# x and v of step 1 loaded three units ahead, sums written over v, small filter tables placed behind E

## The chip, the cores and the metric

The kernel runs on one core of a Trainium2 chip. The metric is device time in microseconds (us); the median of three runs of the kernel before is 1146.1 us (1141.72 to 1146.43). Engines are named as in the profile: PE (TensorE matmul), PEld (its weight loads), DVE (VectorE), ACT (ScalarE), POOL (GpSimd), SP (SyncE, which issues nearly all DMAs of this kernel; SPq is its queue).

## The reference

Two parts, the second fed by the first. All in float32.

```python
# x, v: (4, 11456, 128); pos_emb: (11456, 64); w1: (64, 64); w2: (64, 128)
h = (np.maximum(pos_emb @ w1, 0) @ w2) * np.exp(-0.01 * pos)[:, None]   # a filter
y = irfft(rfft(x * v, 2S, axis=1) * rfft(h, 2S, axis=0))[:, :S]         # long convolution
a = (x * y).reshape(B * S, D)                                           # 45824 tokens
logits = a @ phi                                                        # 32 slots, 8 experts
slot_in = softmax(logits, axis=0).T @ a
slot_out = per expert: relu(slot_in @ w1[e]) @ w2[e]
return softmax(logits, axis=1) @ slot_out
```

## The kernel before

The convolution is a transform of length 111 x 197, done as matrix products in float32. The 128 channels are worked in 8 groups of 16; with 4 batches a group has 64 columns, handled as 16 *units* of 4 columns.

- **Opening** (group-free): 14 loads `pos` feed `hid_step` (the small network of the filter), then `first` with the table `tab1h`, then `filter_second`. The small tables `tab1h`, `w1s`, `w2s`, `wins` are used only up to `filter_last` in group 0.
- **Step 1**, per unit u of group g: `p1_load` loads x and v (224 KB each), multiplies them (POOL, in group 0 every third on DVE), and makes the sum and the difference of the two halves on DVE (`sd`, two instructions, L203). `p1` multiplies sd by `tab1x` on PE (L126, 8 PE instructions a unit) and the result is brought to T, mainly by ACT (L130, L131, L135).
- **Step 2** (`p2`, per 4 frequencies k): a product with W (L218), two multiplications with the filter on DVE (L223), two combinations on POOL (L229, L230) back into T.
- **Step 3** (`p3`, two calls a unit, 16 PE instructions a unit, L236): a product from T, one copy `ec` by ACT (L240) and two DVE instructions into E (L242) a call.
- **Step 4** (`p4`, 7 row blocks, each in two halves): a product of E (L266), multiplied by the gate's x (`xi`, loaded by L254) on DVE (L272) into `xo`, stored to DRAM by `p4_out` (L286, L290, L298).
- After the eight groups the expert part (`Moe`, `_moe`) reads the stored tokens back; the change does not touch its text.

The main loop (L304) runs *passes* g = 0 to 8. A pass has two halves. In the first half step 1 of group g runs unit by unit beside step 3 of group g-1; p1 of a unit writes the places of T that p3 of the same unit reads. In the second half step 4 of group g-1 runs beside step 2 of group g. Pass 0 has no steps 3 and 4, pass 8 no steps 1 and 2.

What sets the order: each engine executes its instructions in the order of its own queue. A scheduler fills the queues when the kernel is built: among the instructions whose inputs and buffers it reckons to be free it takes the one that stands earliest in the text. `inorder` (`tc.keep_in_program_order`) pins an instruction behind the one written before it on the same engine. SP's queue waits at its head: a DMA whose buffer is not free holds back every DMA behind it.

Buffers that matter: pool `ld` has 5 buffers of 2 KB a partition and serves `pos`, x, v (from group 1 on) and `xi`; pool `st` has 3, for `hb` in the opening, sd and `xo`. In group 0 v lies in Hs, a region that the filter values of the later groups use (`hs`, loaded for group g in units 4 to 12 of pass g). E is a region of 15910 floats a partition, of which the steps use 14336 and the opening (hid, F and a ring) 15085. Step 1 is started two units ahead: `p1_load(g, u + 2)` stands before p3 and p1 of unit u.

Of the kernel before, what the change touches and what calls it, by code (L numbers as in the profile page):

```python
# [11 lines left out]
F32 = mybir.dt.float32  # L12
# [5 lines left out]
B, S, D = 4, 11456, 128  # L18

N1, N2 = 111, 197  # L20
L = N1 * N2
J = 99
JT = 105
JP = 112
R = 56
RP = 64
FO = 64
# [32 lines left out]
def conv_part(ctx, tc, cp, moe, xf, vf, xi, pos, w1, w2, win, t1x, t1h, wt, t3, t4, hs, scr):  # L60
    nc = tc.nc
    ld = ctx.enter_context(tc.tile_pool(name="ld", bufs=5))
    st = ctx.enter_context(tc.tile_pool(name="st", bufs=3))
    sm = ctx.enter_context(tc.tile_pool(name="sm", bufs=2))
    psa = ctx.enter_context(tc.tile_pool(name="psa", bufs=4, space=bass.MemoryType.PSUM))
    psb = ctx.enter_context(tc.tile_pool(name="psb", bufs=4, space=bass.MemoryType.PSUM))

    tab1x = cp.tile([JT, 2 * J], F32, tag="tab1x", name="tab1x")
    tab1h = cp.tile([J, 2 * J], F32, tag="tab1h", name="tab1h")
    tab3 = cp.tile([N1, 4 * R], F32, tag="tab3", name="tab3")  # L70
    tab4 = cp.tile([J, 2, N2 + JT], F32, tag="tab4", name="tab4")
    w1s = cp.tile([128, 2 * FO], F32, tag="w1s", name="w1s")
    w2s = cp.tile([128, D], F32, tag="w2s", name="w2s")
    wins = cp.tile([J, R, 2], F32, tag="wins", name="wins")
    W = cp.tile([128, J, N1], F32, tag="W", name="W")


# [3 lines left out]
    Hs = Tall[:, B * 2 * CG * J :].rearrange("p (k x) -> p k x", k=J)  # L81
    moe.E = cp.tile([128, QN * (NSLOT + 1) + 4096], F32, tag="E", name="E")
    E = moe.E[:, : 4 * C * R].rearrange("p (r q c) -> p r q c", q=4, c=C)
    inorder = tc.keep_in_program_order
    RB = 4
    KB = 4
# [98 lines left out]

    def p1_load(g, u):
        xt = ld.tile([JP, 4, 2 * RP], F32, tag="ld", name=f"x_{g}_{u}")
        dma = nc.sync.dma_start(out=xt, in_=xf[g, u])
        if g == 0:
            inorder(dma)  # L190
        if g == 0:

            k = 8 * RP * (u % 5)
            vt = Hs[:JP].rearrange("p k x -> p (k x)")[:, k : k + 8 * RP]
            vt = vt.rearrange("p (c r) -> p c r", c=4)
        else:
            vt = ld.tile([JP, 4, 2 * RP], F32, tag="ld", name=f"v_{g}_{u}")
        nc.sync.dma_start(out=vt, in_=vf[g, u])
        eng = nc.vector if g == 0 and u % 3 == 2 else nc.gpsimd
        inorder(eng.tensor_tensor(out=xt, in0=xt, in1=vt, op=ALU.mult))  # L200
        sd = st.tile([JP, 4, 2 * RP], F32, tag="st", name=f"sd_{g}_{u}")
        for h, op in ((0, ALU.add), (RP, ALU.subtract)):
            add = nc.vector.tensor_tensor(out=sd[:, :, h : h + RP], in0=xt[:, :, 0:RP], in1=xt[:, :, RP:],  # L203
                                          op=op)
            if g == 1:
                inorder(add)
        return sd

    def p1(g, u, sd):
        for h in range(0, 4, 2):  # L210
# [91 lines left out]
    NU = C // 4  # L302

    for g in range(G + 1):  # L304

        if g < G:
            sds = {u: p1_load(g, u) for u in range(2)}
            for u in range(NU):
                if g and 4 <= u < 13:
                    ks = slice(11 * (u - 4), 11 * (u - 3))  # L310
                    inorder(nc.sync.dma_start(out=Hs[:, ks], in_=hs[g, :, ks]))
                if u + 2 < NU:
                    sds[u + 2] = p1_load(g, u + 2)
                if g > 0:
                    p3(g - 1, 4 * u)
                    p3(g - 1, 4 * u + 2)
                p1(g, u, sds.pop(u))
        else:
            moe.weights()
            for u in range(NU):  # L320
                p3(g - 1, 4 * u)
                p3(g - 1, 4 * u + 2)
            moe.places()
# [520 lines left out]
```

## Time and profile before

| what | value |
|---|---|
| median of three runs | 1146.1 us |
| the profiled execution, its own time | 1144.67 us |
| its span (first to last instruction) | 1142.9 us |
| mean granted TensorE clock | 0.967 |
| opening and step 1 of group 0 | 0 to about 125 us |
| step 2 of group 0 | about 125 to 176 us |
| passes 1 to 7, first half / second half | about 52 us / 50 us each |
| pass 8 | about 883 to 937 us |
| expert part | about 937 us to the end |

A row of the timeline reads: start, duration, engine, line, operation, output<-inputs with partitions x elements, how many instructions were merged (x8), and in square brackets how long the engine had been idle and which instruction ended that. Consecutive instructions of a line are merged into one row if nothing of that engine came between. One float32 matmul of the text shows as two PE instructions. A row of the stages (windows) reads: stretch, its length, then busy time and number of instructions for PE, PEld, DVE, ACT and POOL, the granted clock, the busy share of the DMA engines, and GB/s. A row of the waits reads: engine, line, what it waited for: us in total, number of waits, the longest.

### The profile page before, as it was taken

Reading aid. Unit: us, or ns where it says so; the run is one execution under the profiler, and the core shown is the slowest. Engines: PE = TensorE matmul, PEld = TensorE weight load, DVE = VectorE, ACT = ScalarE, POOL = GpSimd, SP = SyncE. Lnnn points to the kernel's source line nnn. Section 1 sums busy time; section 2 is a strip of 40 time slices with the busy share of each in tenths; the row PEclk is TensorE's granted clock in tenths of the full one; section 3 lists DMA queues with packets and bytes.
Section 4 is the critical chain, followed back from the end, with each engine's and each line's share of the span. In section 5 each row is a group of like instructions: output and inputs, shape, how many; then the busy total and the mean of one; then the engine's idle time right before and its main releaser. Section 6 shows DMA issues by size and latency. Waiting matters only on the chain.

```text
span 1142.9 us, 25992 instructions
## 1 busy us (share of the span) xinstructions
PE 1065.8 (93%) x9232; PEld 990.3 (87%) x9232; DVE 878.7 (77%) x1806; ACT 594.7 (52%) x1473; POOL 589.6 (52%) x742
## 2 busy tenths in 40 slices
PE   6998998999999899999999999999999989987997
PEld 6787898999999899989989998998999986655775
DVE  5336667888779688877978787897888839997797
ACT  1978766901840590185049108604920318875697
POOL 6101465266447436743754574375456005776774
PEclk9779998999999999999999999999999989998999
DMA  8423577434824663483357247445824778774388
GB/s 281 132 81 89 183 263 222 146 107 136 237 90 125 184 190 94 141 215 109 117 173 219 76 131 214 127 125 162 231 80 150 234 232 264 228 209 123 137 346 342
DMA packets 129484, 198.44 MB, mean 174 GB/s; under 512 B 15927, under 2 KB 71538, under 8 KB 129357
## 3 DMA queue, kind: packets, MB, share of 16 engines
q1 hardware_dynamic: 129070, 196.61, 55.8%
q8 instruction: 75, 1.23, 0.5%
q14 instruction: 53, 0.43, 0.1%
q10 hardware_dynamic: 254, 0.11, 0.0%
q0 software_dynamic: 32, 0.07, 0.0%
HBM read 136.84 MB, written 59.90 MB: 172 GB/s over the span
## 4 chain that ended last, share of the span: by engine, by line
issue 32%; PE 22%; DVE 16%; DMA 6%; ACT 5%; POOL 3%; SPq 1%; POOLq 0%; DVEq 0%; ACTq 0%
PE p L126 7%; PE p L236 7%; DVE E L242 5%; DMA v<-in_vf_dram 5%; POOL x L200 2%; PE ct L702 2%; DVE xreg L413 2%; DVE sd L203 2%; PE p L266 1%; PE pt L472 1%; DVE xreg L718 1%; DVE ev L539 1%; DVE rd L492 1%; DVE c L679 1%; DVE rm L489 1%
## 5 line engine op out<-in xcount | busy, mean ns | idle before, releaser
L240 ACT ACTIVATE ec<-p 99x224 f32<-99x224 f32 x256 | 83.7, 356 | 396.6 <-issue 338.2
L242 DVE TENSOR_TENSOR E<-p,ec 99x224 f32<-99x224 f32 x512 | 222.3, 553 | 44.9 <-ACT ec L240 44.5
L229 POOL TENSOR_TENSOR T<-m,m 111x256 f32<-111x256 f32 (+1 forms) x200 | 145.2, 726 | 185.6 <-DVE m L223 184.1
L223 DVE TENSOR_TENSOR m<-p,T 111x512 f32<-111x512 f32 (+1 forms) x350 | 216.1, 679 | 23.4 <-issue 16.7
L236 PE MATMUL p<-tab,T 111*99 111x112 f32 x2048 | 222.2, 262 | 6.5 <-POOL T L229 3.0
L200 POOL TENSOR_TENSOR x<-x,v 112x512 f32<-112x512 f32 x112 | 145.0, 1296 | 158.3 <-DMA v<-in_vf_dram 145.4
L236 PEld LDWEIGHTS p<-tab,T 111*99 111x99 f32 x2048 | 215.4, 171 | 11.4 <-POOL T L229 3.2
L266 PE MATMUL p<-E,tab 99*105 99x128 f32 (+1 forms) x1792 | 212.6, 274 | 12.2 <-DVE E L242 12.2
L126 PE MATMUL p<-tab1x,sd 105*128 105x198 f32 x1024 | 201.3, 342 | 18.2 <-DVE sd L203 15.8
L266 PEld LDWEIGHTS p<-E,tab 99*105 99x105 f32 x1792 | 202.6, 172 | 14.4 <-DVE E L242 12.1
L218 PE MATMUL p<-T,W 128*111 128x128 f32 x1584 | 201.4, 279 | 1.1 <-DVE T L133 1.1
L126 PEld LDWEIGHTS p<-tab1x,sd 105*128 105x128 f32 x1024 | 172.1, 194 | 24.9 <-DVE sd L203 15.0
L218 PEld LDWEIGHTS p<-T,W 128*111 128x111 f32 x1584 | 189.8, 176 | 2.9 <-DVE T L133 1.3
L130 ACT ACTIVATE T<-p 64x396 f32<-64x396 f32 x288 | 163.8, 569 | 36.2 <-PE p L126 31.7
L203 DVE TENSOR_TENSOR sd<-x 112x256 f32<-112x256 f32 x256 | 116.2, 494 | 49.3 <-POOL x L200 39.9
L230 POOL TENSOR_TENSOR T<-m,m 111x256 f32<-111x256 f32 (+1 forms) x200 | 145.2, 726 | 0.0
L272 DVE TENSOR_TENSOR xo<-p,xi 105x256 f32<-105x256 f32 x224 | 84.1, 417 | 43.7 <-PE p L266 28.6
L131 ACT ACTIVATE T<-p 64x198 f32<-64x198 f32 x288 | 106.0, 368 | 3.5
L135 ACT ACTIVATE T<-p 64x198 f32<-64x198 f32 x224 | 74.3, 332 | 0.0
L133 DVE TENSOR_SCALAR T<-p 64x198 f32<-64x198 f32 x64 | 27.0, 431 | 45.4 <-ACT T L131 44.0
L520 POOL TENSOR_TENSOR E<-lt,mx 128x480 f32<-128x480 f32 (+1 forms) x24 | 24.6, 1024 | 70.0 <-ACT et L502 66.9
L706 ACT ACTIVATE cs<-ct 96x512 fp32r<-96x512 f32 x96 | 53.3, 567 | 10.2 <-PE ct L702 6.8
(94 smaller groups left out, 1128.3 us busy)
## 6 DMA issues: line engine op xcount, KB each, us to landing
x<-in_xf_dram SPq DMA_DIRECT2D x128, 224.0 KB
v<-in_vf_dram SPq DMA_DIRECT2D x112, 224.0 KB
xi<-in_xi_dram SPq DMA_DIRECT2D x112, 224.0 KB
out_dram<-xreg SPq DMA_DIRECT2D x22, 960.0 KB
xreg<-scr SPq DMA_DIRECT2D x21, 960.0 KB
scr<-xo SPq DMA_DIRECT2D x104, 192.0 KB
hs<-E SPq DMA_DIRECT2D x12, 1024.0 KB
T<-hs SPq DMA_DIRECT2D x63, 176.0 KB
```

The costliest lines, as they stand in the source:

```text
L126: nc.tensor.matmul(ps[:, i].rearrange("p s k -> p (s k)"), lhsT=src(i), rhs=tab, start=True, stop=True)
L130: nc.scalar.activation(to[0:RP], pq[0:RP], AF.Copy)
L131: nc.scalar.activation(to[RP:128, 0], pq[RP:128, 1], AF.Copy)
L200: inorder(eng.tensor_tensor(out=xt, in0=xt, in1=vt, op=ALU.mult))
L203: add = nc.vector.tensor_tensor(out=sd[:, :, h : h + RP], in0=xt[:, :, 0:RP], in1=xt[:, :, RP:], op=op)
L218: nc.tensor.matmul(ps[:, i].rearrange("p b c -> p (b c)"), lhsT=W[:, k0 + i, :], rhs=Tf[:, :, k0 + i, :], start=True, stop=True)
L223: nc.vector.tensor_mul(m[:, :n].rearrange("p k s c i -> p k (s c i)").rearrange("p k (b c) -> p k b c", c=CG), ps[:, :n], h[:, :, CG * s : ...
L229: nc.gpsimd.tensor_tensor(out=Ty[:, 0], in0=ms[0][:, :n, 0], in1=ms[1][:, :n, 1], op=ALU.subtract)
L230: nc.gpsimd.tensor_tensor(out=Ty[:, 1], in0=ms[1][:, :n, 0], in1=ms[0][:, :n, 1], op=ALU.add)
L236: nc.tensor.matmul(ps[:, i, 2 * s : 2 * s + 2, :].rearrange("p q r -> p (q r)"), lhsT=T[0:N1, s, c // CG, c % CG // 2, :, i], rhs=tab3[:, ...
L242: add = nc.vector.tensor_tensor(out=E[:J, :, 2 * s : 2 * s + 2, c : c + 2].rearrange("p r q c -> p c q r"), in0=ps[:, :, 0:2, :], in1=ec, ...
L266: nc.tensor.matmul(ps[:, i, :n], lhsT=tab4[:, s, o : o + JT], rhs=E[:J, r, s : s + 2 * n - 1 : 2, :], start=(s == 0), stop=(s == 1))
```

## The change

- `p1_load` is cut in two: `p1_load` issues the loads, `p1_fold` does the multiplication and the two sums. Loads stand three units ahead, the fold two units ahead as before. At the start of a pass the loads of units 0, 1 and 2 come first, then the folds of 0 and 1.
- Both loads are now pinned (`inorder`) in every group. Before, only x of group 0 was.
- From group 1 on, v is loaded into pool `st`; the sum and the difference are written over v, so that sd has no buffer of its own. In group 0 the same is done in Hs, with six places instead of five.
- Pool `st` has 5 buffers instead of 3.
- `tab1h`, `w1s`, `w2s`, `wins` are no longer tiles of their own; `spare` cuts them from the end of E, behind the ring.

```diff
-    st = ctx.enter_context(tc.tile_pool(name="st", bufs=3))
+    st = ctx.enter_context(tc.tile_pool(name="st", bufs=5))
...
-    tab1h = cp.tile([J, 2 * J], F32, tag="tab1h", name="tab1h")
-    w1s = cp.tile([128, 2 * FO], F32, tag="w1s", name="w1s")
-    w2s = cp.tile([128, D], F32, tag="w2s", name="w2s")
-    wins = cp.tile([J, R, 2], F32, tag="wins", name="wins")
...
+    at = count(J * N1 + 16 * 2 * D)
+
+    def spare(p, n):
+        a = next(at)
+        for _ in range(n - 1):
+            next(at)
+        return moe.E[:p, a : a + n]
+
+    tab1h = spare(J, 2 * J)
+    w1s = spare(128, 2 * FO)
+    w2s = spare(128, D)
+    wins = spare(J, 2 * R).rearrange("p (r h) -> p r h", h=2)
...
     def p1_load(g, u):
         xt = ld.tile([JP, 4, 2 * RP], F32, tag="ld", name=f"x_{g}_{u}")
-        dma = nc.sync.dma_start(out=xt, in_=xf[g, u])
-        if g == 0:
-            inorder(dma)
-        if g == 0:
-
-            k = 8 * RP * (u % 5)
+        inorder(nc.sync.dma_start(out=xt, in_=xf[g, u]))
+        if g == 0:
+
+            k = 8 * RP * (u % 6)
             vt = Hs[:JP].rearrange("p k x -> p (k x)")[:, k : k + 8 * RP]
             vt = vt.rearrange("p (c r) -> p c r", c=4)
         else:
-            vt = ld.tile([JP, 4, 2 * RP], F32, tag="ld", name=f"v_{g}_{u}")
-        nc.sync.dma_start(out=vt, in_=vf[g, u])
+            vt = st.tile([JP, 4, 2 * RP], F32, tag="st", name=f"v_{g}_{u}")
+        inorder(nc.sync.dma_start(out=vt, in_=vf[g, u]))
+        return xt, vt
+
+    def p1_fold(g, u, xt, vt):
+
         eng = nc.vector if g == 0 and u % 3 == 2 else nc.gpsimd
         inorder(eng.tensor_tensor(out=xt, in0=xt, in1=vt, op=ALU.mult))
-        sd = st.tile([JP, 4, 2 * RP], F32, tag="st", name=f"sd_{g}_{u}")
         for h, op in ((0, ALU.add), (RP, ALU.subtract)):
-            add = nc.vector.tensor_tensor(out=sd[:, :, h : h + RP], in0=xt[:, :, 0:RP], in1=xt[:, :, RP:],
+            add = nc.vector.tensor_tensor(out=vt[:, :, h : h + RP], in0=xt[:, :, 0:RP], in1=xt[:, :, RP:],
                                           op=op)
             if g == 1:
                 inorder(add)
-        return sd
+        return vt
...
-            sds = {u: p1_load(g, u) for u in range(2)}
+            xvs = {u: p1_load(g, u) for u in range(3)}
+            sds = {u: p1_fold(g, u, *xvs.pop(u)) for u in range(2)}
             for u in range(NU):
                 if g and 4 <= u < 13:
                     ks = slice(11 * (u - 4), 11 * (u - 3))
                     inorder(nc.sync.dma_start(out=Hs[:, ks], in_=hs[g, :, ks]))
+                if u + 3 < NU:
+                    xvs[u + 3] = p1_load(g, u + 3)
                 if u + 2 < NU:
-                    sds[u + 2] = p1_load(g, u + 2)
+                    sds[u + 2] = p1_fold(g, u + 2, *xvs.pop(u + 2))
```

## Prediction

> **What bounds the kernel now.** I read the page first, for shares, then the list of waits, then the stages, and last the timelines of one pass.
>
> ```profile
> PE 1065.8 (93%) x9232; PEld 990.3 (87%) x9232; DVE 878.7 (77%) x1806; ACT 594.7 (52%) x1473; POOL 589.6 (52%) x742
> ```
>
> ```profile
> PE p L126 7%; PE p L236 7%; DVE E L242 5%; DMA v<-in_vf_dram 5%; POOL x L200 2%; PE ct L702 2%; DVE xreg L413 2%; DVE sd L203 2%; PE p L266 1%; PE pt L472 1%; DVE xreg L718 1%; DVE ev L539 1%; DVE rd L492 1%; DVE c L679 1%; DVE rm L489 1%
> ```
>
> The second line is the chain that ended last. The loads of v, POOL's multiplication and the sums stand on it with 5, 2 and 2 per cent, some 100 us. That is not what the change can win: PE is busy 93% of the span, so most links of that chain run beside a PE that is at work. The waits say what PE itself lost.
>
> ```profile
> POOL x L200 <- DMA v<-in_vf_dram: 145.4, 92, 4.4
> ...
> DVE sd L203 <- POOL x L200: 39.9, 41, 2.5
> ...
> PE p L126 <- DVE sd L203: 15.8, 13, 2.5
> ```
>
> (The columns are total us, number of waits, the longest.) POOL waits 145 us for v, DVE 40 us for POOL, but PE waits only 15.8 us for the sums. 15.8 us is the first ceiling.
>
> ```profile
> 481.00:532.00 51.00, 46.83 (x371) 45.40 (x372) 38.50 (x93) 43.82 (x126) 19.44 (x15) 1.00 0.69 187
> 532.00:582.00 50.00, 49.89 (x434) 49.69 (x434) 41.94 (x80) 0.56 (x2) 35.90 (x51) 0.97 0.37 112
> ```
>
> These are the two halves of pass 4 (PE, PEld, DVE, ACT, POOL busy; clock; DMA share; GB/s). In the second half PE is idle 0.1 us: nothing to win. In the first it is idle 4.2 us, and ACT, busy 43.8 of 51 us, is the next in line. So the question is where in the first half those 4.2 us lie.
>
> ```profile
> 478.00 2.90 PE L236 MATMUL p<-tab,T 111*99 111x112 f32 x24
> 481.04 1.61 PE L126 MATMUL p<-tab1x,sd 105*128 105x198 f32 x8
> 482.48 5.15 PE L236 MATMUL p<-tab,T 111*99 111x112 f32 x48
> 489.40 1.61 PE L126 MATMUL p<-tab1x,sd 105*128 105x198 f32 x8 [1.77 <-DVE sd L203]
> ...
> 530.82 2.37 PE L266 MATMUL p<-E,tab 99*105 99x64 f32 x16 [1.39 <-DVE E L242]
> ```
>
> PE begins the pass with step 3 (L236), which needs no loads, does unit 0 of step 1 (L126) at 481.04, fills with three more units of step 3, and then stands 1.77 us because unit 1 has no sums. The other large gap, 1.39 us, is the end of the half, behind E; the change does not touch it.
>
> **Start of passes 2 to 7, the main term.** I take these six passes as alike. Why unit 1 is late in pass 4:
>
> ```profile
> 468.15 0.42 SPq L188 DMA_DIRECT2D x<-in_xf_dram x1
> ```
>
> ```profile
> 480.17 0.25 SPq L298 DMA_DIRECT2D scr<-xo  x1
> 480.46 0.32 SPq L198 DMA_DIRECT2D v<-in_vf_dram  x1
> ...
> 520.70 3.36 SPq L254 DMA_DIRECT2D xi<-in_xi_dram  x5
> ```
>
> ```profile
> 478.45 1.27 POOL L200 TENSOR_TENSOR x<-x,v 112x512 f32<-112x512 f32 x1
> 483.80 1.29 POOL L200 TENSOR_TENSOR x<-x,v 112x512 f32<-112x512 f32 x1 [4.08 <-DMA v<-in_vf_dram]
> ```
>
> ```profile
> 484.73 2.94 DVE L242 TENSOR_TENSOR E<-p,ec 99x224 f32<-99x224 f32 x7 [1.74 <-ACT ec L240]
> ...
> 487.53 1.82 DVE L203 TENSOR_TENSOR sd<-x 112x256 f32<-112x256 f32 x2
> ```
>
> With five `ld` buffers for x, v and xi, v of unit 1 finds one only at 480.46, lands 3.3 us later, is multiplied until 485.09, and its sums then stand behind seven instructions of step 3 on DVE.
>
> What the two adds and a unit's share of step 3 cost on DVE when little is in the way shows in pass 1:
>
> ```profile
> 193.63 1.79 DVE L203 TENSOR_TENSOR sd<-x 112x256 f32<-112x256 f32 x2
> 195.35 1.75 DVE L242 TENSOR_TENSOR E<-p,ec 99x224 f32<-99x224 f32 x4
> 196.92 0.76 DVE L203 TENSOR_TENSOR sd<-x 112x256 f32<-112x256 f32 x2
> ```
>
> The change gives x all of `ld` and v all of `st`, so six loads can go in a row. But it also pins x of unit 0 behind the last store of `p4_out`, the row at 480.17. Today that load went at 468.15, twelve microseconds earlier, past two rounds of stores. So unit 0 moves back: x at about 480.5, v at 480.9, landing by 484.2 (the same 3.3 us), multiplied by 485.5, summed by 486.3 (two adds at 0.76): p1 of unit 0 at 486.3 or later instead of 481.04. Unit 1 follows one pair of loads behind; at one multiplication, 1.3 us, to one and a half, its p1 comes near 487.8, against 489.40 today. PE has something to do meanwhile: from 478.0 to 486.3 about five units of step 3, which DVE clears in 1.75 us each. What was late is therefore replaced by something almost as late: unit 1 is 1.6 us earlier, and of that I count 1.2 us a pass, because the opening of the half becomes one block of waiting instead of two. Six passes: **-7.2 us**. Bounds: the whole gap goes (6 x -1.77 = -10.6), or the pass gets worse because ACT has nothing of step 1 to clear until unit 0 arrives. ACT's work for half a unit of step 1:
>
> ```profile
> 500.29 0.54 ACT L130 ACTIVATE T<-p 64x396 f32<-64x396 f32 x1
> ...
> 501.44 0.54 ACT L130 ACTIVATE T<-p 64x396 f32<-64x396 f32 x1
> ```
>
> From one to the next are 1.15 us, so a unit is 2.3 us of ACT, and ACT is the second most loaded engine here. If one unit's worth is lost at the start and not made up, that is +2 us a pass, +12 us in all. SP's other queue entries are passed by nothing new: xi stays unpinned.
>
> **Pass 1.** Its first loads went during group 0, so it shows what a pass without the late start looks like, and what the pin costs.
>
> ```profile
> 179.89 3.01 PE L126 MATMUL p<-tab1x,sd 105*128 105x198 f32 x8 [0.46 <-DVE sd L203]
> 182.69 2.35 PE L236 MATMUL p<-tab,T 111*99 111x112 f32 x16
> 184.88 1.52 PE L126 MATMUL p<-tab1x,sd 105*128 105x198 f32 x8
> 186.23 1.70 PE L236 MATMUL p<-tab,T 111*99 111x112 f32 x16
> 187.77 1.52 PE L126 MATMUL p<-tab1x,sd 105*128 105x198 f32 x8
> ```
>
> ```profile
> 167.31 7.82 SPq L159 DMA_DIRECT2D hs<-E  x3
> ```
>
> Units alternate every 2.89 us (184.88 to 187.77) with no gap. After the change x of unit 0 is pinned behind the last store of hs, so it goes at 175.1 at the earliest; with 0.4 + 3.3 + 1.3 + 0.8 its sums are ready at 180.9 instead of 179.9, later if the stores hold up the load. In pass 1 the sums are pinned ahead of step 3 on DVE as well, so those of unit 2 hold up E. **+2 us**; bounds 0 and +6.
>
> **Group 0.** Of the 15.8 us that PE waits for sums, 6 x 1.77 and 0.46 lie in the passes above; 4.7 us are left, in group 0 and in small pieces. Six places for v and five for x, none for sd, let six units be summed before PE comes to them, instead of three. ACT sets the pace there, so not all of it counts: **-2 us**, bounds 0 and -4.7. The opening:
>
> ```profile
> 3.86 0.33 SPq L198 DMA_DIRECT2D T<-in_vf_dram  x1
> ```
>
> ```profile
> 20.12 1.96 PE L109 MATMUL ph<-w1s,pos 128*99 128x128 f32 x16 [1.33 <-DMA pos<-in_pos_dram]
> ```
>
> v of group 0, written far behind, slips between the loads of pos; pinned, it no longer can. PE waited 1.33 us for a pos: **-0.7 us**, bounds 0 and -1.3.
>
> **The rest.** Tables behind E: the same transfers to another address, nothing overlaps the ring that ends where they begin; cost nil, covered by the first loads. Sums over v: same instructions, shapes and count. Five `st` buffers: in pass 8 one xo waited for a store.
>
> ```profile
> 933.56 0.76 DVE L272 TENSOR_TENSOR xo<-p,xi 105x256 f32<-105x256 f32 x2 [0.45 <-DMA scr<-xo]
> ```
>
> **-0.45 us**, bounds 0 and that.
>
> Sum: -7.2 + 2 - 2 - 0.7 - 0.45 = -8.35. The profiled execution took 1144.67 us, so 1136.3; the median of the runs is 1.4 us above it, so **about 1138 us**. All lower bounds give 1144.67 - 17.1 + 1.4 = 1129, all upper ones 1144.67 + 18 + 1.4 = 1164. A measurement of this kernel can tell about 0.5%, 5.7 us, from no change.
>
> **Rivals.**
>
> *All the idle time of the first halves goes.* Then passes 2 to 7 look like pass 1 and each gains the 4.2 us of the stage row: -25 us, 1121. For it: pass 1. Against it: the pin, and the 1.39 us at the end.
>
> *Nothing moves* (1146). The pin eats in each pass what the deeper loads give; unit 0 is as late as unit 1 was. The trace allows it: the p1 of 489.40 and the one I put at 486.3 to 487.8 differ by less than the 2.4 us that the sums stood behind E on DVE.
>
> *Slower: xi takes x's buffers.* At 520.70 five loads of xi go at once, for three row blocks, as soon as five `ld` buffers are free: loads that are ready take what is free. Today x and v are as ready as xi and stand earlier, so they win. Pinned, x of unit u+3 stands behind v of u+2, which waits for a p1, and at the end of a pass behind `p4_out`; a buffer that falls free then goes to xi and stays there until step 4. It decides when x is left with one buffer: a unit then costs 0.4 + 3.3 + 1.3 + 0.8 = 5.8 us in series instead of 2.9; with two it is 2.9, a draw. Eight units of group 0 at 2.9 us more are 23 us; in passes 1 to 7 steps 3 and 4 fill most of the time, and I take a tenth of the like 23 us in each, 16 us: +39 us, about 1185.
>
> *Slower: POOL and DVE get in each other's way.* The same two adds take 0.76 us at 196.92 and 1.79 us at 193.63. The slow row is from pass 1, where multiplications run ahead of the sums. DVE needs 1.75 + 0.76 = 2.51 us a unit against PE's 2.89; it becomes the bound when the sums lose more than 0.38 us on average. At the full 1.03 us of the row, 0.65 us x 16 units x 7 passes = +73 us, 1219; at half of it +15 us, 1161. Against it: pass 1 has such a row, and PE kept its 2.89. The Trainium skill, "SBUF — State Buffer", section "SBUF: two separate sides", states that GpSimd and a DVE instruction with two SBUF inputs lock each other out for a whole instruction; the extra 1.03 us, near one multiplication of 1.27, agrees. By that rule the change, which lets the multiplication run ahead of the sums in every pass, could only cost here.
>
> **How the numbers follow.** Forecast 0.44, of which 0.34 ends below 1140.4 and 0.10 within 0.5%; all idle gone 0.08; nothing moves 0.14; xi 0.22; POOL and DVE 0.12. Faster 0.42, same 0.24, slower 0.34. The range reaches from just under the best case, 1120, to just over the xi case, 1190; it leaves out most of the POOL case and half of the spread above 1185, together 0.19.
>
> **What would show it.** Right: at the start of passes 2 to 7 no load of x before the last `scr<-xo`, then six loads in a row; p1 of unit 0 six or more us after the first L236, with five units of L236 ahead of it, and the next p1 without a gap over 1 us; second halves unchanged; no v before the last pos. Wrong: L254 rows among the first loads of a pass, or before pass 1 (xi); L203 pairs mostly above 1.2 us (POOL); L126 of unit 0 after 489 in every pass (nothing moves); first L126 at 481 or earlier (the pin does not hold).

## The result, and the profile after

The changed kernel is slower by 1%: the median is 1156.41 us (1147.84 to 1173.07, 16 runs) against 1143.69 us (1135.65 to 1154.91, 16 runs) for the kernel before, ratio 1.0103 with a 95% interval of 1.0076 to 1.013. The forecast of 1138 us had the wrong sign, and the time lies in the range on the side of the rivals. The first profile was taken in a slow execution (1173.07 us, clock 0.949), which the ratio leaves out, so the profile shown here is that of a later run of the same kernel, whose execution took 1153.42 us with a span of 1151.7 us.

Line numbers have moved: of the changed kernel, L197 and L205 load x and v, L211 is the multiplication, L213 the two sums, L135 step 1 on PE, L246 step 3, L250 and L252 its `ec` and E, L276 step 4.

The page, busy time and then the chain that ended last by line:

```profile
PE 1069.8 (93%) x9232; PEld 990.8 (86%) x9232; DVE 906.2 (79%) x1806; ACT 596.0 (52%) x1473; POOL 594.6 (52%) x742
...
PE p L276 10%; PE p L228 10%; PE p L246 6%; PE p L135 6%; DVE E L252 6%; DMA v<-in_vf_dram 3%; ACT T L139 3%; DVE v L213 3%; ACT T L140 2%; PE ct L715 2%; DVE xreg L426 2%; DVE rd L505 1%; DVE xreg L731 1%; DVE ev L552 1%; ACT T L144 1%
```

The instruction counts are those of before. Only DVE's busy time has moved by more than 1%: 906.2 us instead of 878.7. The waits (total, number, longest):

```profile
POOL x L211 <- DMA v<-in_vf_dram: 126.0, 82, 6.3
...
PE p L135 <- DVE v L213: 17.0, 18, 1.6
...
DVE v L213 <- POOL x L211: 16.0, 8, 7.0
...
DVE T L213 <- POOL x L211: 4.5, 2, 3.4
...
PE p L135 <- DVE T L213: 1.4, 1, 1.4
```

In this kernel the sums of group 0 appear under the name T, those of the later groups under v; before, both were sd. DVE waits for POOL 20.5 us in all (7.0 of it at one place, the start of pass 1) instead of 39.9: the products are ready earlier, as the change says. PE nevertheless waits for the sums no less than before, 18.4 us against 15.8. The two halves of pass 3:

```profile
385.00:437.00 52.00, 46.03 (x365) 44.35 (x363) 43.28 (x95) 43.16 (x125) 21.43 (x16) 1.00 0.73 199
437.00:484.00 47.00, 47.00 (x421) 47.00 (x422) 40.83 (x77) 0.96 (x3) 34.09 (x49) 1.00 0.33 99
```

In the first half PE is idle 6 us of 52, and DVE, 38.5 us in the like stretch of pass 4 before, is now as loaded as ACT: 43.28 us. PE's rows of that half:

```profile
382.46 9.43 PE L246 MATMUL p<-tab,T 111*99 111x112 f32 x92
393.20 1.61 PE L135 MATMUL p<-tab1x,v 105*128 105x198 f32 x8 [1.32 <-DVE v L213]
...
395.05 1.61 PE L135 MATMUL p<-tab1x,v 105*128 105x198 f32 x8
398.08 1.58 PE L135 MATMUL p<-tab1x,v 105*128 105x198 f32 x8 [1.42 <-ACT T L144]
...
417.83 1.58 PE L135 MATMUL p<-tab1x,v 105*128 105x198 f32 x8 [0.58 <-DVE v L213]
419.24 0.93 PE L246 MATMUL p<-tab,T 111*99 111x112 f32 x8
421.07 0.99 PE L246 MATMUL p<-tab,T 111*99 111x112 f32 x8 [0.90 <-DVE E L252]
...
436.99 1.94 PE L276 MATMUL p<-E,tab 99*105 99x64 f32 x16 [1.58 <-DVE E L252]
```

The gaps stand at three places: at the late start, as foreseen; in the middle of the half, where nothing was foreseen; and at its end, behind E. What DVE and POOL did at the first two:

```profile
384.31 7.30 DVE L252 TENSOR_TENSOR E<-p,ec 99x224 f32<-99x224 f32 x18 [0.90 <-ACT ec L250]
391.45 1.70 DVE L213 TENSOR_TENSOR v<-x 112x256 f32<-112x256 f32 x2
...
415.75 1.82 DVE L213 TENSOR_TENSOR v<-x 112x256 f32<-112x256 f32 x2
417.50 0.93 DVE L252 TENSOR_TENSOR E<-p,ec 99x224 f32<-99x224 f32 x2
418.26 1.83 DVE L213 TENSOR_TENSOR v<-x 112x256 f32<-112x256 f32 x2
...
420.77 1.81 DVE L213 TENSOR_TENSOR v<-x 112x256 f32<-112x256 f32 x2
```

```profile
391.26 1.27 POOL L211 TENSOR_TENSOR x<-x,v 112x512 f32<-112x512 f32 x1 [1.42 <-DMA x<-in_xf_dram]
...
416.02 1.28 POOL L211 TENSOR_TENSOR x<-x,v 112x512 f32<-112x512 f32 x1 [1.07 <-DVE E L252]
418.55 1.27 POOL L211 TENSOR_TENSOR x<-x,v 112x512 f32<-112x512 f32 x1 [1.25 <-DVE E L252]
420.86 1.44 POOL L211 TENSOR_TENSOR x<-x,v 112x512 f32<-112x512 f32 x1 [1.04 <-DMA v<-in_vf_dram]
```

Each of these four pairs runs beside a multiplication that began just before it or during its first sum, and takes 1.70 to 1.83 us instead of the 0.76 quoted in the prediction; the multiplications take 1.27 to 1.44 us. Three such pairs stand one behind another at 415.75, 418.26 and 420.77, and PE's gaps of the middle follow them. At the start, at 391.45, the sums of unit 0, late already behind eighteen instructions of step 3, are lengthened by the multiplication of unit 1 as well.

Pass 1, SP's queue and then PE:

```profile
165.76 10.68 SPq L168 DMA_DIRECT2D hs<-E  x4
176.53 0.85 SPq L197 DMA_DIRECT2D x<-in_xf_dram  x1
177.43 1.18 SPq L205 DMA_DIRECT2D v<-in_vf_dram  x1
```

```profile
177.56 6.47 PE L246 MATMUL p<-tab,T 111*99 111x112 f32 x32 [2.98 <-POOL T L239]
185.64 6.04 PE L135 MATMUL p<-tab1x,v 105*128 105x198 f32 x22 [1.60 <-DVE v L213]
```

The first load of the pass leaves right behind the last store of the filter, and step 1 begins 8.1 us after step 3 instead of 3.6.

A table of stages for all kernels stands behind the experiments. For the changed kernel it has three profiles; their means against before: pass 1 begins at 176.1 us (before 176.3), its first half takes 55.6 us (51.1), the first halves of passes 2 to 7 together 320.8 us (318.8), the second halves of passes 1 to 7 together 335.0 us (335.0). At the end of step 3 in pass 8 these sum to 6.5 us behind. That is all that the profiles hold: the three spans are 1149.3 us on average against 1142.9. The medians are 9 to 13 us apart, but the three profiled executions took 2.3 us less on average than the medians of their runs, and the one of before 1.0 us more than its median; single executions of the changed kernel differ by more than 10 us. What is left between the two is not placed.

### The profile page after: what moved, and what is told of

Same layout as the page of the kernel before. It is cut to its first block, busy times and chain, and to the rows that moved or that the text cites. A ratio compares the mean times of both kernels' runs of the same rounds, so it can differ in the third digit from the quotient of the medians.

```text
span 1171.3 us, 26100 instructions
## 1 busy us (share of the span) xinstructions
PE 1084.1 (93%) x9232; PEld 1007.3 (86%) x9232; DVE 915.3 (78%) x1806; ACT 596.0 (51%) x1473; POOL 595.5 (51%) x742
## 3 DMA queue, kind: packets, MB, share of 16 engines
q8 instruction: 75, 1.23, 0.5%
## 4 chain that ended last, share of the span: by engine, by line
PE 40%; DVE 17%; issue 11%; ACT 8%; DMA 5%; POOL 3%; SPq 1%; ACTq 0%; DVEq 0%; POOLq 0%
PE p L276 10%; PE p L228 10%; PE p L135 8%; PE p L246 6%; DVE E L252 6%; ACT T L139 3%; DVE v L213 3%; DMA v<-in_vf_dram 2%; ACT T L140 2%; PE ct L715 2%; DVE xreg L426 1%; PE pt L485 1%; ACT ec L250 1%; DVE xreg L731 1%; DVE rd L505 1%
## 5 line engine op out<-in xcount | busy, mean ns | idle before, releaser
L250 ACT ACTIVATE ec<-p 99x224 f32<-99x224 f32 x256 | 85.7, 356 | 400.5 <-issue 343.2
L252 DVE TENSOR_TENSOR E<-p,ec 99x224 f32<-99x224 f32 x512 | 218.3, 549 | 51.4 <-ACT ec L250 51.4
L246 PE MATMUL p<-tab,T 111*99 111x112 f32 x2048 | 222.3, 263 | 9.2 <-DVE E L252 4.9
L211 POOL TENSOR_TENSOR x<-x,v 112x512 f32<-112x512 f32 x112 | 148.8, 1331 | 156.9 <-DMA v<-in_vf_dram 119.9
L246 PEld LDWEIGHTS p<-tab,T 111*99 111x99 f32 x2048 | 214.8, 172 | 15.5 <-issue 7.9
L276 PE MATMUL p<-E,tab 99*105 99x128 f32 (+1 forms) x1792 | 215.7, 276 | 13.4 <-DVE E L252 13.4
L276 PEld LDWEIGHTS p<-E,tab 99*105 99x105 f32 x1792 | 205.2, 173 | 15.7 <-DVE E L252 13.3
L228 PE MATMUL p<-T,W 128*111 128x128 f32 x1584 | 205.0, 282 | 0.6 <-DVE T L142 0.6
L135 PE MATMUL p<-tab1x,v 105*128 105x198 f32 x896 | 183.5, 351 | 22.1 <-DVE v L213 15.4
L228 PEld LDWEIGHTS p<-T,W 128*111 128x111 f32 x1584 | 193.8, 180 | 2.4 <-DVE T L142 0.8
L135 PEld LDWEIGHTS p<-tab1x,v 105*128 105x128 f32 x896 | 156.5, 201 | 27.6 <-DVE v L213 13.8
L213 DVE TENSOR_TENSOR v<-x 112x256 f32<-112x256 f32 x224 | 143.0, 684 | 19.8 <-POOL x L211 17.1
L142 DVE TENSOR_SCALAR T<-p 64x198 f32<-64x198 f32 x64 | 27.4, 432 | 53.1 <-ACT T L140 52.3
L719 ACT ACTIVATE cs<-ct 96x512 fp32r<-96x512 f32 x96 | 53.3, 567 | 10.4 <-PE ct L715 7.1
```

The source lines that it names most:

```text
L135: nc.tensor.matmul(ps[:, i].rearrange("p s k -> p (s k)"), lhsT=src(i), rhs=tab, start=True, stop=True)
L213: add = nc.vector.tensor_tensor(out=vt[:, :, h : h + RP], in0=xt[:, :, 0:RP], in1=xt[:, :, RP:], op=op)
L228: nc.tensor.matmul(ps[:, i].rearrange("p b c -> p (b c)"), lhsT=W[:, k0 + i, :], rhs=Tf[:, :, k0 + i, :], start=True, stop=True)
L246: nc.tensor.matmul(ps[:, i, 2 * s : 2 * s + 2, :].rearrange("p q r -> p (q r)"), lhsT=T[0:N1, s, c // CG, c % CG // 2, :, i], rhs=tab3[:, ...
L252: add = nc.vector.tensor_tensor(out=E[:J, :, 2 * s : 2 * s + 2, c : c + 2].rearrange("p r q c -> p c q r"), in0=ps[:, :, 0:2, :], in1=ec, ...
L276: nc.tensor.matmul(ps[:, i, :n], lhsT=tab4[:, s, o : o + JT], rhs=E[:J, r, s : s + 2 * n - 1 : 2, :], start=(s == 0), stop=(s == 1))
```

## The experiments

Three theories. **A**: the pins make the loads of each pass late, and that alone costs the time. **B**: POOL's multiplications, running ahead, lengthen DVE's sums, which hold up PE directly or through E. **C**: xi takes the load buffers of x. Ratios are to the kernel before on the same chip, with 95% intervals. "Pairs beside a multiplication" were counted from the timelines of DVE and POOL, groups 1 to 7, for rows of exactly two sums that overlap a multiplication by more than 0.05 us; pairs that stand in longer rows are not counted (27 of 112 in the profile after, 2 before).

**The changed kernel again, three times.**

> The changed kernel as it is, for an undisturbed profile. Both theories expect the 1.010 of the first measurement (1.007 to 1.013) and, in the profile, the first halves of passes 2 to 7 longer than before (52.8 us in pass 4) by about 1.5 us, and that of pass 1 by more. Theory A (the late start by the pins) expects PE's gaps and ACT's idle time to lie in the first 12 us of each pass; theory B (POOL's multiplications beside DVE's sums) expects the sums' busy time, 0.49 us each before, at about 0.68 us, and the loss at the end of each first half, behind E.

1153.16 us, 1.0103 (1.0066 to 1.0141).

> The changed kernel unchanged, on the chip of the next three runs, so that what the chain takes off is measured side by side, and for another profile of a kernel whose executions differ by more than 10 us. Theory B: the ratio is 1.007 to 1.013 again, pairs of sums beside a multiplication at 1.2 to 1.6 us, and first halves of passes 2 to 7 that differ from pass to pass by one to four us as the overlaps fall; if the profile shows them all alike, the spread is not the sums.

1152.6 us, 1.0071 (1.0042 to 1.01).

> The changed kernel unchanged, for the same chip as the next three: 1.007 to 1.011 by both theories.

1154.15 us, 1.0101 (1.0059 to 1.0144).

In the profile of the second of these runs 29 pairs have no multiplication beside them and take 0.74 us (0.72 to 0.76); 56 have one and take 1.43 us (0.74 to 2.63). Before, it was 78 at 0.75 and 32 at 1.23. The groups of the sums, busy time and mean ns of one, before and then after:

```profile
L203 DVE TENSOR_TENSOR sd<-x 112x256 f32<-112x256 f32 x256 | 116.2, 494 | 49.3 <-POOL x L200 39.9 <-PE p L126 8.4
```

```profile
L213 DVE TENSOR_TENSOR v<-x 112x256 f32<-112x256 f32 x224 | 134.6, 647 | 16.0 <-POOL x L211 16.0
L213 DVE TENSOR_TENSOR T<-x 112x256 f32<-112x256 f32 x32 | 15.4, 508 | 5.1 <-POOL x L211 4.5
```

Together 150.0 us for 128 units, 1.17 us a unit (1.10 and 1.13 in the other two profiles), against 116.2 us before, 0.91 a unit. The first halves of passes 2 to 7 differ by 2 us within this profile (52.5 to 54.5), as B expected. Two things that B had expected did not come in the first of the three profiles: the first halves of passes 2 to 7 were no longer than before (53.0 us against 53.1), and the sums took 0.55 us each, not 0.68. C is refuted: behind the last store of a pass the queue has x and v of units 0 to 4 in turn, and loads of xi only behind x of unit 15. SP's queue in pass 3:

```profile
384.60 0.25 SPq L308 DMA_DIRECT2D scr<-xo  x1
384.89 0.32 SPq L197 DMA_DIRECT2D x<-in_xf_dram  x1
385.31 0.38 SPq L205 DMA_DIRECT2D v<-in_vf_dram  x1
...
419.44 0.31 SPq L205 DMA_DIRECT2D v<-in_vf_dram  x1
420.16 9.88 SPq L264 DMA_DIRECT2D xi<-in_xi_dram  x5
```

**The pins alone**, on the kernel before:

```diff
-        dma = nc.sync.dma_start(out=xt, in_=xf[g, u])
-        if g == 0:
-            inorder(dma)
+        inorder(nc.sync.dma_start(out=xt, in_=xf[g, u]))
...
-        nc.sync.dma_start(out=vt, in_=vf[g, u])
+        inorder(nc.sync.dma_start(out=vt, in_=vf[g, u]))
```

> The kernel before with every load of x and v pinned, and nothing else: old buffers, two units ahead, sums in a buffer of their own. Theory A: the pins alone make it late; x of unit 0 goes behind the last store of the pass before, and with only two units ahead nothing is won back: ratio 1.010 to 1.025. Theory B: the sums still follow their multiplication, 0.49 to 0.55 us each, and the time stays within 0.5% of before.

1163.78 us, 1.0194 (1.0168 to 1.022). A's number, and B's expectation failed: with old buffers and loads two ahead the pins cost twice what the whole change costs. But it does not show that lateness alone did it, because the sums lengthened too:

```profile
L201 DVE TENSOR_TENSOR sd<-x 112x256 f32<-112x256 f32 x256 | 134.1, 564 | 51.3 <-POOL x L198 41.7 <-PE p L126 8.4
```

134.1 us against 116.2, with 53 pairs beside a multiplication at 1.39 us. That the pins bunch the loads, and bunched loads put multiplications beside sums, is a reading; the pins with short sums were not run on the kernel before, so its 20 us are not divided between lateness and overlap.

**Early loads, pins kept.** The first three pairs of loads stand ahead of step 4 of the last row block (two more places, not shown, keep group 0 as it was and do the same for pass 1, ahead of the last three stores of the filter):

```diff
+            if t == 6 and g + 1 < G:
+                xvs = {u: p1_load(g + 1, u) for u in range(3)}
             for h in range(2):
                 p4(g - 1, rb, xs, h, xo)
```

> The changed kernel with the first three pairs of loads of a pass written, and so pinned, ahead of step 4 of the last row block of the pass before (for pass 1: ahead of the last three stores of the filter). Pins, buffers and sums over v stay. Theory A: unit 0 is ready when the pass begins, the loss at the start goes: ratio to before 0.985 to 1.000, first half of pass 4 at 52 us or less, of pass 1 at 52 to 54. Theory B: the multiplications run still further ahead of the sums; ratio 1.008 to 1.015 as in the changed kernel, sums at 0.68 us or more.

1163.55 us, 1.02 (1.0168 to 1.0232). Step 1 now begins 5.9 to 7.5 us after step 3 instead of about 10, and the first halves of passes 2 to 7 are longer, 55.6 us on average. A is refuted for these passes: the start came earlier and the time did not follow. Part of the 55.6 us is the clock. In every one of these six halves the trace shows a granted clock of 0.50 for 3.4 or 6.8 us in all; in the first of them here (the clock is the third number from the end):

```profile
296.81:303.60 6.79, 6.52 (x22) 6.48 (x23) 6.07 (x14) 3.91 (x11) 3.33 (x3) 0.50 0.68 176
```

Half of that time, 13.7 us over the six halves, is lost to it, against 0, 0 and 1.7 us in the three profiles of the changed kernel. Without it the six halves come to 319.9 us, against 320.3: starting 4 us earlier gained nothing. The run is worse than B expects, though the sums are as long as in the first profile of the changed kernel (604 ns each from group 1 on); POOL's multiplications here stood behind E on DVE for 38.6 us in all, against 14.1 there:

```profile
POOL x L211 <- DVE E L252: 38.6, 17, 7.1
```

Why they did is not settled.

**The chain: a multiplication waits for the sums before it.** The product gets a tile of its own with one buffer:

```diff
-        inorder(eng.tensor_tensor(out=xt, in0=xt, in1=vt, op=ALU.mult))
+        pr = sm.tile([JP, 4, 2 * RP], F32, tag="pr", name=f"pr_{g}_{u}", bufs=1)
+        inorder(eng.tensor_tensor(out=pr, in0=xt, in1=vt, op=ALU.mult))
...
-            add = nc.vector.tensor_tensor(out=vt[:, :, h : h + RP], in0=xt[:, :, 0:RP], in1=xt[:, :, RP:],
+            add = nc.vector.tensor_tensor(out=vt[:, :, h : h + RP], in0=pr[:, :, 0:RP], in1=pr[:, :, RP:],
```

> The changed kernel with the product written to a tile of its own with one buffer, so that the multiplication of a unit waits until the sums of the unit before have read it: POOL and DVE can't work on neighbouring units at the same time. Theory A: the start stays as late, and the time with it, 1.010 (or a little more, for the chain adds waits). Theory B: the sums fall back to 0.5 us and with them DVE's busy time by some 35 us; ratio 0.995 to 1.003.

1135.24 us, 0.9935 (0.9912 to 0.9957), against 1153.16 us for the changed kernel on the same chip.

> The changed kernel with the chained product, unchanged, beside the next run. The stages of the profiles say that it gains 0.5 us a pass over the kernel before with the chain and loses 5 us in pass 1: no difference that can be measured. The ratios of two different chips said 0.9935 against 0.9996. If the ratios are right, it is again 0.5% ahead.

1137.0 us, 0.9934 (0.991 to 0.9958), against 1152.6.

> The product in a tile with one buffer, unchanged, on this chip: 0.991 to 0.996. The distance to the run with two buffers is what the remaining overlap of multiplications and sums costs.

1137.21 us, 0.995 (0.9925 to 0.9975), against 1154.15. So 16 to 18 us go, three times, and B stands; two of the three ratios are lower than the 0.995 that B had as its best. In the profile of the second of these runs, DVE and POOL at the start of pass 3, then PE at the end of the half:

```profile
385.06 0.76 DVE L214 TENSOR_TENSOR v<-pr 112x256 f32<-112x256 f32 x2
...
394.02 0.76 DVE L214 TENSOR_TENSOR v<-pr 112x256 f32<-112x256 f32 x2 [1.44 <-POOL pr L212]
396.22 0.76 DVE L214 TENSOR_TENSOR v<-pr 112x256 f32<-112x256 f32 x2 [1.44 <-POOL pr L212]
```

```profile
392.72 1.27 POOL L212 TENSOR_TENSOR pr<-x,v 112x512 f32<-112x512 f32 x1 [0.93 <-DVE v L214]
394.92 1.27 POOL L212 TENSOR_TENSOR pr<-x,v 112x512 f32<-112x512 f32 x1 [0.93 <-DVE v L214]
```

```profile
428.04 1.94 PE L277 MATMUL p<-E,tab 99*105 99x64 f32 x16 [0.99 <-DVE E L253]
```

POOL and DVE take turns, 2.20 us a unit (394.02 to 396.22), under the 2.89 us that PE needs. That looks like a loss, since DVE waits 1.44 us for each product; but all 112 pairs take 0.71 to 0.76 us, and DVE's busy time is 857.5 us instead of 906.2. Every first half of passes 2 to 7 takes 51.9 to 52.2 us. The order of the work did not change: from pass 1 on, PE, DVE, ACT and POOL execute their instructions in the same order as in the changed kernel, and SP's queue holds the same loads and stores in the same order.

**The same chain on the kernel before.** Same edit, sums still into sd.

> The kernel before with the product in a tile of its own with one buffer and nothing else, so that here too a multiplication waits for the sums of the unit before. Theory B (POOL's multiplications lengthen DVE's sums) expects every pair of sums at 0.75 us and the sums' busy time down by some 20 us. If the deeper loads of the change are worth nothing by themselves, the ratio is 0.993, the same as for the changed kernel with this chain; if they are worth the 1.2 us a pass that that kernel's first halves gained, it is 0.997 to 1.003, because with five buffers for x and v unit 1 still waits for its v.

1138.82 us, 0.9996 (0.9975 to 1.0017). The sums did what B expected: all 112 pairs at 0.72 to 0.77 us, busy 96.8 us instead of 116.2.

> The kernel before with the chained product, unchanged, beside the run above: within 0.3% of it if the stages are right, 0.5% or more behind it if the ratios are right.

1141.24 us, 0.9975 (0.9954 to 0.9996), beside 1137.0 for the changed kernel with the chain on that chip: 0.37% behind, between the two expectations. So keeping the sums short is worth 0 to 0.25% before the change and 1.4 to 1.7% after it. The stages say where the small rest lies: with short sums in both, the first halves of passes 2 to 7 take 52.4 and 52.5 us with the old buffers and 51.9 to 52.0 with the new ones.

**What the chain does: no overlap, or x's buffer free earlier?** The product tile also frees x before the sums. With two product buffers that stays, and a multiplication may again run beside the sums of the unit before; from pass 1 on, the order of the instructions on every engine is the same as with one buffer.

> The changed kernel with the product in a tile of its own again, but with two buffers instead of one: x's buffer is free as early as with the chain, while a multiplication may again run beside the sums of the unit before. Theory B (the overlap costs): pairs of sums beside a multiplication at 1.2 to 1.5 us again, first halves of passes 2 to 7 at 52.5 us or more, ratio 1.003 to 1.012. If what the chain gained came from x's buffer being free earlier: 0.990 to 0.996, first halves at 52 us.

1143.73 us, 1.0006 (0.9976 to 1.0035): between the two, a little below B's 1.003.

> The product in a tile with two buffers, unchanged, beside the changed kernel and the chain on one chip. If the 1.0006 holds against 1.007 to 1.011, half of the chain's gain comes without keeping multiplications and sums apart: 1.000 to 1.003. If it was the chip: within 0.3% of the run above.

1145.47 us, 1.0018 (0.9992 to 1.0043), with the changed kernel at 1154.15 and one buffer at 1137.21 on the same chip. Half of the gain comes with two buffers already. Seven load buffers instead of five, product in place:

> The changed kernel with seven load buffers instead of five (the two more take the place that the two product tiles took), product in place as in the change. If x's buffer being held until the sums is the other half, seven buffers undo that as the product tile did: 0.999 to 1.004. If what the product tile did is to let a multiplication run one unit ahead at most, seven buffers don't help: 1.006 or more, with pairs of sums beside a multiplication as long as in the changed kernel.

1153.17 us, 1.0084 (1.005 to 1.0117): no better than the changed kernel, so it isn't x's buffer. What remains is how far a multiplication may run ahead: as far as the loads allow 1154 us, one unit 1145, not at all 1137. This is an inference from what is left; no run moves the distance and nothing else. The overlap that is left with two buffers is milder, 44 and 48 pairs at 1.21 and 1.26 us in its two profiles, against 51, 56 and 56 at 1.34, 1.43 and 1.41 in the changed kernel's three.

**Without the pins.** The pins of before (only x of group 0) in the changed kernel, and then with the chain as well:

> The changed kernel with the pins of before (only x of group 0); buffers, loads three ahead and sums over v stay. If the pins cost the time, 0.990 to 1.003. If the lengthened sums cost it, they are there with free loads too: 1.005 to 1.015, pairs of sums beside a multiplication at 1.2 to 1.4 us. If xi takes the buffers of x once the pins are gone, or had to be kept away by them, loads of xi stand among the first loads of a pass and it is 1.02 or more.

1146.61 us, 1.0066 (1.0035 to 1.0096).

> The same without the pins, with the chained product. If pins and lengthened sums each cost on their own, it is faster than the changed kernel with the chain alone (0.9935): 0.980 to 0.990, first units of a pass at 5 us or less after the first product of step 3. If the pins cost nothing once the sums are short, 0.992 to 0.996.

1135.28 us, 0.996 (0.9939 to 0.9981). The first expectation, that the pins cost the time, is refuted: free loads begin step 1 after 4 us and leave a loss, with 57 pairs beside a multiplication at 1.28 us. And once the sums are short the pins of passes 2 to 7 cost nothing: 52.1 us a first half without them, 51.9 to 52.0 with. They do cost pass 1: its first half takes 51.8 us without pins and 54.7 to 56.5 with (50.2 against 53.2 to 54.9 with the chain). So by these profiles 3 to 5 us of the changed kernel's loss are the pin's in pass 1; the ratios, 1.0066 against 1.0071 to 1.0103, have intervals that overlap and do not show it. The profiled execution without pins, 1137.6 us, was the fastest of its twelve, whose median is 1146.61; its row in the table below is a good case.

**Pass 1 with early loads**, chain and pins kept; the first three pairs of group 1 go ahead of the last three stores of the filter.

> The changed kernel with the chain, and the first three pairs of loads of group 1 ahead of the last three stores of the filter (as in the run with early loads, for this one pass). Its first half of pass 1 takes 54.9 us against 51.9 in the later passes. If the late loads make these 3 us: 52 to 53 us, ratio 0.990 to 0.992. If the order of the sums in pass 1 makes them (there they are pinned ahead of step 3 on DVE): still 54 to 55 us, ratio 0.9935.

1135.66 us, 0.9976 (0.9954 to 0.9998). The first half of pass 1 falls to 49.3 us, so it is the late loads that make it long. The ratio of 0.990 to 0.992 that was to come with it did not come: the pass begins at 181.2 us instead of 176.3, behind one wait of PE for the end of step 2 that is 3.0 us in the changed kernel and 3.1 with the chain alone:

```profile
PE p L247 <- POOL T L240: 6.4, 1, 6.4
```

The 4 to 6 us were given back ahead of the place where they were won.

**The best of it**: the chain from group 1 on only, and no pins for the loads of group 1 (the edit for v, not shown, is that for x):

```diff
+        pr = xt
+        if g:
+            pr = sm.tile([JP, 4, 2 * RP], F32, tag="pr", name=f"pr_{g}_{u}", bufs=1)
...
-        inorder(nc.sync.dma_start(out=xt, in_=xf[g, u]))
+        dma = nc.sync.dma_start(out=xt, in_=xf[g, u])
+        if g != 1:
+            inorder(dma)
```

> The changed kernel with the chained product from group 1 on only (in group 0, where DVE takes every third product, the chain delayed the end of the pass by some 2 us), and without the pins on the loads of group 1 alone. Pass 1 begins at 174 to 176 and its first half takes 50 to 52 us, passes 2 to 7 keep 51.9: some 4 us less than with the chain alone, ratio 0.988 to 0.993. If the lengthened sums of group 0 or free loads in pass 1 cost as much as this saves, it equals the chain alone.

1130.46 us (1128.34 to 1133.32), 0.9881 (0.9856 to 0.9906): faster than both kernels, 6.5 us ahead of the chain alone on the same chip. PE at the start of pass 1:

```profile
175.84 3.29 PE L253 MATMUL p<-tab,T 111*99 111x112 f32 x16 [2.82 <-POOL T L246]
178.93 2.08 PE L135 MATMUL p<-tab1x,v 105*128 105x198 f32 x8
180.84 1.70 PE L253 MATMUL p<-tab,T 111*99 111x112 f32 x16
```

Units alternate without a gap from the first on, and the pass begins no later than before.

**The stages of all profiles**, from PE's rows. A first half runs from the first product of step 3 to the first of step 4, a second half from there to the next step 3. "Long" counts second halves of over 48 us among seven (the others take 47.2 to 47.5). Where no number of profiles is given it is one.

| kernel | pass 1 begins | its first half | first halves 2 to 7, mean (lowest to highest) | long second halves |
|---|---|---|---|---|
| before | 176.3 | 51.1 | 53.1 (52.5-53.9) | 3 |
| changed, three profiles | 174.2, 177.6, 176.6 | 55.8, 56.5, 54.7 | 53.0, 53.5, 53.9 (52.5-55.2) | 3, 4, 2 |
| before, pins alone | 173.8 | 54.9 | 55.4 (53.0-58.8) | 4 |
| changed, early loads | 179.9 | 53.3 | 55.6 (54.7-56.3) | 1 |
| changed, no pins | 175.0 | 51.8 | 52.8 (51.0-53.9) | 1 |
| changed, seven load buffers | 176.1 | 54.8 | 53.6 (53.2-54.0) | 6 |
| changed, two product buffers, two profiles | 176.3, 175.3 | 54.5, 55.6 | 52.6, 52.9 (52.1-53.6) | 2, 4 |
| changed, chain, three profiles | 176.3, 176.3, 176.6 | 54.9, 53.5, 53.2 | 51.9, 52.0, 51.9 (51.9-52.2) | 0, 0, 0 |
| changed, chain, no pins | 178.3 | 50.2 | 52.1 (52.0-52.4) | 2 |
| before, chain, two profiles | 176.7, 178.1 | 49.9, 50.4 | 52.4, 52.5 (51.8-53.4) | 1, 1 |
| changed, chain, pass 1 early | 181.2 | 49.3 | 52.0 (51.9-52.1) | 0 |
| best | 175.8 | 49.3 | 52.0 (51.9-52.2) | 0 |

## Why the prediction was wrong

The step that failed is "Sums over v: same instructions, shapes and count", which enters the sum with nothing. The sums have the same shape and another duration, 1.17 us a unit instead of 0.91, because products that are ready early mean multiplications beside sums. With the overlap taken away by the chain, 16 to 18 us go. In the profiles some 9 of these lie in the first halves of passes 2 to 7 (320.8 us to 311.8), 2 in pass 1, and 5 in the second halves, where the chain's three profiles show no drop of the clock; the kernel before paid the same 5. The prediction had the mechanism as its last rival, with both rows quoted, and gave it 0.12.

- **Start of passes 2 to 7** (-7.2 us taken, +2.0 measured in the mean of three profiles). With the overlap taken away these halves come to 51.9 us and the six of them to -7 us, the number taken. That agreement is partly chance: the chain on the kernel before has 4.2 us of it already (3.4 of them are two drops of the granted clock to 0.50, for 3.4 us each, in the one profile of before), and the deeper loads by themselves are worth 0.5 us a pass, 3 us in all, not 1.2 a pass. The picture of the start held: x goes right behind the last store, and step 3 runs 92 of PE's instructions ahead (5.75 units, five foreseen). Step 1 began 9.8 to 10.9 us after step 3, where 8.3 was foreseen, because the sums of unit 0 stood behind eighteen instructions of step 3 on DVE, which the sum left out for unit 0 while it had named the like for unit 1. The mark "the next p1 without a gap over 1 us" all but held (at most 1.02, in unit 1), but the p1 behind that, of unit 2, waited 1.42 us in pass 3 and up to 1.70 elsewhere; with the chain it waits 0.80.
- **Pass 1** (+2, bounds 0 and +6): +4.5 us in the mean (3.6 to 5.3), inside the bounds, by the mechanism named, the pin behind the stores of the filter. The prediction named all that made it larger and sized it too small: the first load left at 176.53 instead of 175.1, the load of v behind it took 1.18 us to issue, and three pairs of sums went ahead of step 3 on DVE.
- **Group 0 and opening** (-2.7): pass 1 begins at 174.2, 177.6 and 176.6 us against 176.3; no gain can be told from the spread. No load of v stands before the last pos any more, as foreseen.
- **st buffers** (-0.45): the wait of xo for a store is gone in two of the three profiles; in the third xo waits once for a store, 5.0 us. **Tables behind E**: no run took them alone; nothing in the profile points to them.
- **Rivals.** "Nothing moves" describes passes 2 to 7 in the best of the three profiles (53.0 against 53.1 us), by another cause than it gave. The xi rival did not happen, nor did it without the pins. The POOL and DVE rival is what happened. That its "half" case (+15 us) is near the 12 to 13 us measured is partly luck, for 4.5 of these are the pin in pass 1. Its condition was too simple: the sums lose 0.34, 0.41 and 0.37 us a unit on average in the three profiles, about the 0.38 from which it was to decide, so its formula gives 3 us at most (0.03 x 16 x 7). The loss comes in rows of lengthened sums, as at 415.75 to 420.77; that PE has too few units in hand to wait for the average is the reading of these rows, not a separate test. Its mark, "L203 pairs mostly above 1.2 us", would have missed it too: 39, 46 and 42 of the 112 pairs are, against 15 before. The argument against it ("PE kept its 2.89") rested on a single pair; what it needed was the count of pairs that the change would put beside a multiplication. It went from 32 to 51, 56 and 56.
- The Trainium skill, "SBUF — State Buffer", section "SBUF: two separate sides", was read rightly: by that rule the overlap could only cost, the measured sign is that of the rule, and with no overlap the time falls below that of the kernel before (0.9934 to 0.995). The prediction had read it and gave the rival 0.12 all the same.

## What to carry to other kernels

When a producer on POOL is let run ahead of a consumer on DVE, look not only at who waits for whom but at what they then do at the same time: a wait that is removed may have been what kept the two engines apart. Count the instructions that will newly overlap, at the duration that the slow rows of the trace show, before a gain is booked. Here a buffer count of one, which makes the engines take turns, was worth more than all the deeper loads: 9 us against 3 in the first halves of passes 2 to 7.

## What the runs showed of the hardware

**Which instructions lengthen.** Of DVE's instructions in passes 1 to 7 only the sums, whose two inputs both lie in SBUF, get longer beside POOL. Step 3's additions into E, with one input in PSUM, keep their duration: in the profile after, 185 of them overlap POOL's work by more than 0.1 us and take 556 ns on average, the other 327 take 554. In pass 1 four of them, 1.72 us in all:

```profile
198.45 1.72 DVE L252 TENSOR_TENSOR E<-p,ec 99x224 f32<-99x224 f32 x4
```

```profile
199.50 1.27 POOL L211 TENSOR_TENSOR x<-x,v 112x512 f32<-112x512 f32 x1 [1.60 <-DVE E L252]
```

The Trainium skill, "SBUF — State Buffer", section "SBUF: two separate sides", has DVE instructions with two SBUF inputs take part in the lock, against a GpSimd instruction that reads SBUF; the sums and the additions into E agree.

Which of the two began first decides who waits. In the profile after, ten pairs have one multiplication that begins between the start of the first sum and that of the second, and take 1.81 to 1.86 us; ten have one that begins during the second sum, and take 0.73 to 0.76 us, while these multiplications take 1.27 to 1.52 us. The sums lose more, because one of them is 0.4 us long and a multiplication 1.27: over all 112, a multiplication takes 1.32 us on average in the first profile of the changed kernel and 1.28 in the first with the chain.

**Behind a short gap of PE the clock can drop.** A second half takes 47.2 or about 48.8 us, and the difference is the granted clock in its first few us. Two second halves of the profile after, PE's first rows and then the clock (third number from the end) in stretches of 3.4 and 4 us:

```profile
436.99 1.94 PE L276 MATMUL p<-E,tab 99*105 99x64 f32 x16 [1.58 <-DVE E L252]
...
537.84 2.36 PE L276 MATMUL p<-E,tab 99*105 99x64 f32 x16 [1.68 <-DVE E L252]
```

```profile
539.22:542.62 3.40, 3.40 (x19) 3.40 (x18) 1.37 (x4) 0.00 (x0) 0.00 (x0) 0.50 0.00 0
437.00:441.00 4.00, 4.00 (x36) 4.00 (x37) 2.12 (x5) 0.96 (x3) 0.00 (x0) 1.00 0.00 0
```

Half of 3.4 us, 1.7 us, is about the difference. Of the 126 second halves in the 18 profiles of the table, 62 began after a gap of less than 1.39 us on PE, and none of them was long; 64 began after 1.39 us or more, and 34 of these took 48.7 to 50.4 us (1.39 us is the shortest gap ahead of a long one). In the three profiles of the changed kernel the gap behind E is 1.4 to 1.5 us on average, with the chain 1.0 to 1.1, so part of what the chain saves is saved here: in the second profiles of the two on the same chip, 6.4 us of the 16.7 us between the spans (four long halves against none). That the gap is the cause is not shown, only that none of these second halves was long without it; nearly half of those with such a gap were not long either. The Trainium skill, "TensorE: Matmul & The Clock Gate", section "Why this matters for your kernels", advises against idle gaps of more than about 3 us; here drops came with half of that.
